# Attention and a squared-ReLU MLP in one kernel: v read as fp32 by SyncE's queue and cast on GpSimd, weight sums on GpSimd, batch 2's x turned by DMA

## The chip, the cores and the metric

The kernel runs on one core of a Trainium2 chip. The metric is device time in microseconds for one execution; lower is better. Engines are called as in the profile: PE (TensorE, matrix products; PEld is its loading of weights), DVE (VectorE), ACT (ScalarE), POOL (GpSimd), SP (SyncE, which here only issues DMAs).

## The reference, cut to what matters

```python
B, H, S, D = 8, 8, 576, 64
scores = q @ k.T / sqrt(D) + bias[bucket(|i - j|)]       # per batch and head, 576 x 576
attn   = exp(scores) / sum(exp(scores))
x      = (attn @ v)            -> 4608 tokens x 512
h      = maximum(x @ w_in, 0)                             # 512 -> 2048
out    = (h * h) @ w_out                                  # 2048 -> 512, fp32
```

All inputs and the output are fp32 in memory; the kernel computes in fp16 with fp32 accumulation.

## The kernel before, in words

**Attention.** Work goes by *pairs*: pair p = 4·b + hp is two heads of batch b, 32 pairs in all. `pair` does one. q and k of both heads are turned so that the head's 64 values lie on partitions (for batches 0 to 2 by PE, L608, with a copy out of PSUM, L570 on ACT or L572 on DVE; from batch 3 on by DMA transposes of SP's queue, L591). Scores come from L653 (four key tiles, 512 queries), L677 (last 64 queries) and L702 (last 64 keys); the last two need `qz`, small zero-padded copies made on POOL or DVE (L635). ACT takes the exponentials (L664, L687, L712). The bias enters as a factor: DVE multiplies the exponentials near the diagonal by a table of exp(bias) (`tb_sb`, `tm_sb`; L745, called the bands). PE then multiplies by v (L781, L788, into the one PSUM bank `pv`), in two halves of three and two query tiles; v carries a column of constants so that the row sums come along. DVE takes a reciprocal (L805) and scales (L810) into `x`. x is turned into `xt` for the next layer: for batches 0 to 2 by PE, four tiles into a bank (`x_turn`, L848) and a copy; from batch 3 on by DMA.

**MLP.** Tokens go in nine groups g of 512 (`layers`). Layer 1 is 16 *atoms* of four 128x512 products (L1044, called f1 here), each with a ReLU (L1065 on ACT, L1067 on DVE) and a square (L1075, DVE). Layer 2 of a group (`second`, L962) is a 2x2 block product done with seven products in place of eight, 14 atoms of eight 128x256 products. It needs sums of the activations' blocks (L921, DVE) and sums of w_out's blocks, made once (`sums_of_weights`, L901, eight DVE instructions of 128x1024, the results in `wt_sb` and in place in `w_out_sb`). Results leave through `y` and SP's queue (L1015).

**Loads.** q, k, v and the weights come through POOL's DMA queue, which casts fp32 to fp16 on the way (L271). v of batch 0 comes by heads (`load_v_head`), of the others by token tiles (`load_v`), always as fp16 straight into `va` (tokens 0 to 511) and `vm` (the last 64). Only pair 0's q and k come as fp32 over SP's and ACT's queues into the room of a later buffer, `first_f`, and are cast by ACT and DVE.

**Order.** Everything is recorded in a planner (`Plan`). Each operation has a time it is estimated to take, a due time, buffers (`Ring`, with so many slots) and earlier operations it depends on. The planner fixes the order of each engine's queue before the kernel runs: of what could start earliest it takes what is due first. `nominal(p)` is a pair's due time, `G0` and `GP` give the groups' due times, `AHEAD` says how early a pair may begin. On the chip each engine runs its list in order and waits on semaphores, so the planner's times matter only through the order that they make. Operations put down as `DMA` are transfers that the planner expects, not instructions.

Of the kernel before, what the change touches and what calls it, by code (L numbers as in the profile page):

```python
# [30 lines left out]
PERIOD, LEAD, FAST, FASTN = 9600.0, 1600.0, 3000, 7  # L31
AHEAD, G0, GP = 20600.0, 54700.0, 35900.0
DT_X = 3
RELU_DVE = 2
NSTG, NQK, NPT, NV, NX, NGB, NRT, NY = 5, 4, 3, 3, 6, 2, 4, 4
QUIET, LATER = 5200.0, 8500.0
TAB, EV = 6400.0, 1
P_ORDER = "1 6 2 5 7 3 4"
P_LAST = "1 6 2 5 7 3 4"
SIX = 3  # L40
ORDER = "k0 i0 q0 q1 v i1 i2 o0 k1 o1 i3 o2 o3"
# [149 lines left out]
def kernel(  # L191
# [38 lines left out]
    one_sb = sb("one_sb", [1, 128], FP32)  # L230
    ex_sb = sb("ex_sb", [128, 8])
    eb_sb = sb("eb_sb", [128, 4, 8])
    oh_sb = sb("oh_sb", [128, 512])
# [14 lines left out]
    gs = [sb(f"g{i}", [128, 16, GT]) for i in range(NGB)]  # L248
    rts = [sb(f"rt{i}", [128, GT]) for i in range(NRT)]
# [16 lines left out]
    def loader(eng_name, eng, out_, in_, packets, deps=(), bufs=(), due=0.0):  # L266

        lane = [Buf(r_lane)] if eng_name == "POOL" else []
        issue = P.add(
            {eng_name: 720.0 if eng_name == "POOL" else 600.0},  # L270
            lambda: io(eng.dma_start(out=out_(), in_=in_())),  # L271
            deps,
            list(bufs) + lane,
            due,
        )
        return P.add({"DMA": packets / 16}, None, [issue], list(bufs) + lane, due if lane else -1e9), issue
# [9 lines left out]
    def load(eng_name, eng, out_, in_, packets, deps=(), bufs=(), due=0.0):  # L286
        return loader(eng_name, eng, out_, in_, packets, deps, bufs, due)[0]
# [15 lines left out]
        128 * 27, due=0,  # L303
# [21 lines left out]
        {"PE": 250.0},  # L325
# [21 lines left out]
    for c in range(6):  # L347
        t_b = Buf(r_g)

        def t_mm(c=c, t_b=t_b):  # L350
            for j in range(16 * c, 16 * c + 16):
                io(
                    nc.tensor.matmul(  # L353
                        g_ps[t_b.slot][:, ts(j - 16 * c, 32)], oh_sb[:, 380 - 4 * j : 508 - 4 * j],
                        eb_sb.rearrange("p i h -> p (i h)"), start=True, stop=True,
                    )
                )

        o = P.add({"PE": 16 * 55.0}, t_mm, [o_eb, l_oh], [t_b], LEAD + TAB, 0.0, "f")

        def t_ev(o, c=c, t_b=t_b):
            src = g_ps[t_b.slot].rearrange("p (w h) -> p h w", h=H)
            dst = tb_sb[:, :, ts(c, 64)]
            if o.eng == "ACT":
                io(nc.scalar.activation(out=dst, in_=src, func=COPYF))
            else:
                io(nc.vector.tensor_copy(out=dst, in_=src))

        tabs_done.append(one_of({"DVE": dve(512), "ACT": act(512)}, t_ev, [o], [t_b], 1.0))
# [17 lines left out]
    def fill(ap, value, ns, due, after, deps=()):  # L387
# [3 lines left out]
    z_fix = [[fill(zz[:, 0], 0.0, 150.0, 10, QUIET)], [fill(zz[:, 1:], 0.0, 300.0, 11, LATER)]]  # L391
    first = [
        fill(pt_sb[:, :, PW:], 1.0, 150.0, 20, LATER),
        fill(pm_sb[:, :, S:], 1.0, 150.0, 20, LATER),
# [11 lines left out]
        fill(stg[i][w][96:128, 512:640].bitcast(FP32), 0.0, 90.0, 40 + i, 25000.0)  # L406
# [4 lines left out]


# [50 lines left out]
    def cast_first(w):  # L463

        def cast(o):
            src, dst = first_f[0:96, ts(w, 768)], stg[b_stg[0].slot][w][0:96, :]
            if o.eng == "ACT":
                io(nc.scalar.activation(out=dst, in_=src, func=COPYF))
            else:
                io(nc.vector.tensor_copy(out=dst, in_=src))  # L470

        l_qk[0, w] = [one_of({"ACT": act(768), "DVE": dve(768, 2.0)}, cast, [l_first[w]], [b_stg[0]], -3.0)]

    def load_v_head(b, h):
        l = load(
            "POOL", nc.gpsimd,
            lambda: vas[b_v[b].slot][:, :, h, 0:64],
            const(v[b, h, 0:512, :].rearrange("(t p) d -> p t d", p=128)),
            512 * 34.5, v_fix[min(b, 1)], [b_v[b]], pdue(),
        )  # L480
        l_v.setdefault((b, h // 2), []).append(l)
# [12 lines left out]
    def load_v(b):  # L494
        for tt in range(4):
            l = load(
                "POOL", nc.gpsimd,
                lambda tt=tt: vas[b_v[b].slot][:, tt, :, 0:64],
                const(v[b, :, ts(tt, 128), :].transpose([1, 0, 2])),
                1024 * 34.5, v_fix[min(b, 1)], [b_v[b]], pdue(),  # L500
            )
            for hp in range(4):
                l_v.setdefault((b, hp), []).append(l)
        load_v_tail(b)

# [22 lines left out]
    for hp in range(4):  # L528
        for w in range(2):
            if hp:  # L530
                load_six(hp, w)
            else:
                cast_first(w)
        if hp == 2:
            load_v_tail(0)
        if hp >= 1:
            for h in range(2 * hp - 2, 2 * hp):
                load_v_head(0, h)
    for h in range(6, 8):
        load_v_head(0, h)  # L540
    for step in ORDER.split():
        if step[0] == "i":
            load_w_in(int(step[1]))
        elif step[0] == "o":
            load_w_out(int(step[1]))
        elif step[0] in "qk":
            for p in range(4 + 2 * int(step[1]), 6 + 2 * int(step[1])):
                load_six(p, "qk".index(step[0]))
        else:
            load_v(1)  # L550
    for b in range(2, B):
# [3 lines left out]
        load_v(b)  # L555
# [3 lines left out]
    def nominal(p):  # L559
        return LEAD + FAST * min(p, FASTN) + PERIOD * max(p - FASTN, 0)  # L560

    xt_ready, x_last = {}, {}
# [17 lines left out]
    def pair(p):  # L580
# [5 lines left out]
        for w, dst in ((0, qts), (1, kts)):  # L586
# [14 lines left out]
            def tr(w=w, bank=bank):  # L601
                ps = g_ps[bank.slot].bitcast(FP16)
                t = stg[b_stg[p].slot][w]
                if b < SIX:
# [12 lines left out]
            o = P.add({"PE": 12 * 36.0 if b < SIX else 5 * mm(128)}, tr, l_qk[p, w] + [l_id], [bank, b_stg[p]], T - 3000, after, "c" if b < SIX else "f")  # L617
# [153 lines left out]
        for part, qt0, nq in ((0, 0, 3), (1, 3, 2)):  # L771
            bank = Buf(r_pv)

            def pv(qt0=qt0, nq=nq, bank=bank):
                ps = pv_ps[bank.slot][:, 0 : nq * 130].rearrange("p (t e d) -> p t e d", t=nq, e=2)
# [27 lines left out]
            def recip(nq=nq, bank=bank, rb=rb):  # L803
                ps = pv_ps[bank.slot][:, 0 : nq * 130].rearrange("p (t e d) -> p t e d", t=nq, e=2)
                io(nc.vector.reciprocal(out=rs[rb.slot][:, 0:nq], in_=ps[:, :, :, 64:65]))  # L805

            def norm(nq=nq, bank=bank, rb=rb, qt0=qt0):
                ps = pv_ps[bank.slot][:, 0 : nq * 130].rearrange("p (t e d) -> p t e d", t=nq, e=2)
# [29 lines left out]
    def x_turn(b, norms):  # L838
        xb = [x_bufs[4 * b + hp] for hp in range(4)]
        T = nominal(4 * b + 3)  # L840
        for qt in range(5):
            n = 128 if qt < 4 else 64
            bank = Buf(r_g)

            def tr(qt=qt, bank=bank):
                ps = g_ps[bank.slot].bitcast(FP16)
                for kk in range(4):
                    io(nc.tensor.transpose(ps[:, ts(kk, 128)], xs[xb[kk].slot][:, qt, :], id_sb))  # L848

            deps = [n_[0 if qt < 3 else 1] for n_ in norms]  # L850
            o = P.add({"PE": 4 * mm(128)}, tr, deps, [bank] + xb, T, 0.0, "f")
            t0 = (b % XB) * S + qt * 128
            for a, z in [(0, n)]:
                c = t0 + a
                e = copy_to(
                    4 * (z - a),
                    lambda a=a, z=z, c=c: xt_sb[:, :, c : c + z - a],
                    lambda a=a, z=z, bank=bank: g_ps[bank.slot].bitcast(FP16)[:, 0:512].rearrange(
                        "p (k t) -> p k t", k=4
                    )[:, :, a:z],  # L860
                    [o] + xt_free(b * S + qt * 128 + n), [bank], T,
                )
                for g_ in range((b * S + qt * 128) // GT, (b * S + qt * 128 + n - 1) // GT + 1):
                    xt_ready.setdefault(g_, []).append(e)
# [19 lines left out]
    def sums_of_weights():  # L884

        done = []
        for c0 in (0, 4):
            cs = ds(c0, 4)
            l = [l_wout[c0 // 2], l_wout[c0 // 2 + 1]]
# [3 lines left out]
            for out_, a, b_, op in (  # L893
# [6 lines left out]
                    {"DVE": dve(1024, 2.0)},  # L900
                    lambda out_=out_, a=a, b_=b_, op=op: io(nc.vector.tensor_tensor(out=out_, in0=a, in1=b_, op=op)),  # L901
                    l + [o], (), 1e5,
# [123 lines left out]
    def layers(g):  # L1026
# [4 lines left out]
        if g < NG:  # L1031
# [3 lines left out]
            for nt in range(16):  # L1035
                bank = Buf(r_g)

                def f1(nt=nt, bank=bank):
                    c = (g * GT) % XR
                    n = min(GT, XR - c)  # L1040
                    for a, z, c in ((0, n, c), (n, GT, 0)):
                        for kk in range(4 if z > a else 0):
# [11 lines left out]
        for i in range(16):  # L1054
            if i < len(atoms1):
                nt, f1, bank = atoms1[i]
                o = P.add(
                    {"PE": 4 * mm(512)}, f1, xt_ready[g] + [l_win[nt // 4]], [bank, gb1], due + i * 2000, 0.0, "f"
# [38 lines left out]
    for b in range(B):  # L1097
        norms = [pair(4 * b + hp) for hp in range(4)]
        if b < DT_X:
            x_turn(b, norms)  # L1100
# [38 lines left out]
```

The softmax here doesn't subtract the row's maximum and nothing guards it: scores larger than these inputs give would overflow.

## Time and profile before

| | |
|---|---|
| time, median of 3 runs | 377.3 us (377.29 to 378.32) |
| the profiled execution | 378.11 us |
| its span, first to last instruction | 376.3 us |
| PE busy in the span | 362.4 us |
| DVE, ACT, POOL busy | 269.0, 255.5, 178.3 us |
| first f1 product starts | 41.24 us |
| DMA packets of POOL's queue (q0) | 94496, 60.9% of 16 engines' span |
| DMA packets of SP's and ACT's queues (q1) | 51280, 27.3% |

The span is that of the instructions; the time of the execution is 1.8 us longer. [...] A window row gives, for a stretch of the span, each engine's busy time and number of instructions, the clock granted to PE, the share of DMA time and the rate. POOL's DMA rows are the issue of a transfer; the transfer itself lands some us later.

### The profile page before, as it was taken

What the parts mean: (1) busy time and instruction counts of PE and PEld (TensorE: products, weight loads), DVE (VectorE), ACT (ScalarE), POOL (GpSimd) and SP (SyncE); (2) the same over time, 40 slices, a digit from 0 to 9 for tenths busy, and PEclk for the clock granted to TensorE, in tenths of its full rate; (3) what the DMA queues carried; (4) which work ended last, traced back from release to release, by engine and by line L of the source; (5) the groups of instructions that cost most, each with busy time, mean ns of one, the idle gap of its engine ahead of it and who ended that gap; (6) DMA issues with size and microseconds to landing.
All of it is one profiled execution on the core that took longest, in us unless ns stands there. A gap on an engine that the chain in (4) does not pass through costs nothing.

```text
span 376.3 us, 10050 instructions
## 1 busy us (share of the span) xinstructions
PE 362.4 (96%) x4046; PEld 247.6 (66%) x4046; DVE 269.0 (71%) x612; ACT 255.5 (68%) x361; POOL 178.3 (47%) x318
## 2 busy tenths in 40 slices
PE   3988999999999999999999999999999999999996
PEld 2656555745778666687766765677577878556775
DVE  3987689998788677767685777757776683583653
ACT  4888979988557887866787778747885541564330
POOL 7876453889368583933758446583550000000000
PEclk9989999999999999999999999999999999999999
DMA  9999999699999999949999799999990222200103
GB/s 171 145 119 159 200 170 88 44 95 84 83 159 129 111 118 145 108 47 119 142 135 67 109 121 149 79 110 105 162 116 30 77 58 68 70 2 28 57 28 111
DMA packets 146163, 38.74 MB, mean 103 GB/s; under 512 B 128070, under 2 KB 146118, under 8 KB 146118
## 3 DMA queue, kind: packets, MB, share of 16 engines
q0 software_dynamic: 94496, 18.07, 60.9%
q1 hardware_dynamic: 51280, 19.75, 27.3%
q8 instruction: 31, 0.51, 0.6%
q10 hardware_dynamic: 342, 0.30, 0.3%
q14 instruction: 14, 0.11, 0.1%
HBM read 36.88 MB, written 9.44 MB: 123 GB/s over the span
## 4 chain that ended last, share of the span: by engine, by line
PE 90%; ACT 4%; DVE 3%; issue 1%; DMA 1%; ACTq 0%
PE f L1044 34%; PE f L962 29%; PE pv L788 10%; PE st L653 9%; PE pv L781 3%; PE st L702 2%; PE st L677 2%; ACT pt L664 1%; PE f L608 1%; DMA g<-in_k_dram 1%; ACT pt L687 1%; PE f L848 1%; DVE x L810 0%; ACT kt L570 0%; PE f L353 0%
## 5 line engine op out<-in xcount | busy, mean ns | idle before, releaser
L664 ACT ACTIVATE pt<-st 128x1024 f16<-128x1024 f32 x128 | 126.8, 1024 | 22.6 <-PE st L653 22.5
L1044 PE MATMUL f<-xt,w_in_sb 128*128 128x512 f16 (+4 forms) x704 | 142.1, 341 | 0.0
L1065 ACT ACTIVATE rt<-f 128x512 f16<-128x512 f32 x134 | 80.0, 598 | 62.0 <-PE f L1044 60.5
L1044 PEld LDWEIGHTS <-w_in_sb 128*128 128x128 f16 x704 | 62.6, 98 | 53.0 <-issue 10.8
L1075 DVE TENSOR_TENSOR g<-rt 128x512 f16<-128x512 f16 x144 | 60.7, 423 | 41.3 <-ACT rt L1065 40.2
L745 DVE TENSOR_TENSOR pt<-pt,tb_sb 128x1536 f16<-128x1536 f16 (+2 forms) x96 | 58.2, 621 | 10.6 <-ACT pt L664 10.2
L962 PEld LDWEIGHTS <-g 128*128 128x128 f16 x576 | 54.9, 98 | 15.4 <-issue 4.7
L788 PE MATMUL pv<-va,pt 128*128 128x65 f16 x1280 | 55.3, 194 | 0.0
L788 PEld LDWEIGHTS <-pt 128*128 128x128 f16 x1280 | 50.9, 98 | 2.9 <-issue 0.7
L271 POOL DMA_DIRECT2D qs<-in_q_dram x71 | 50.0, 725 | 2.4 <-DMA ks<-in_k_dram 1.1
L271 POOL DMA_DIRECT2D ks<-in_k_dram x71 | 50.0, 715 | 1.4 <-issue 1.4
L962 PEld LDWEIGHTS <-s 128*128 128x128 f16 x432 | 40.6, 98 | 10.6 <-issue 3.4
L635 POOL COPY qz<-qt 64x64 f16<-64x64 f16 x53 | 15.5, 293 | 64.2 <-DMA qt<-qs 35.5
L989 DVE SCALAR_TENSOR_TENSOR y<-f,y 128x512 f32<-128x512 f32 (+1 forms) x47 | 31.4, 667 | 16.1 <-PE f L962 15.1
L653 PE MATMUL st<-qt,kt 64*128 64x512 f16 x256 | 41.6, 396 | 1.1 <-ACT pt L664 0.5
L962 PE MATMUL f<-wt,g 128*128 128x256 f16 x288 | 36.6, 273 | 0.0
L962 PE MATMUL f<-w_out_sb,s 128*128 128x256 f16 x288 | 36.6, 273 | 0.0
L962 PE MATMUL f<-w_out_sb,g 128*128 128x256 f16 x288 | 36.2, 273 | 0.1
L781 PE MATMUL pv<-vm,pm 128*128 128x130 f16 x160 | 35.5, 222 | 0.5 <-DVE x L810 0.4
L635 POOL COPY qz<-kt 64x64 f16<-64x64 f16 x59 | 20.2, 342 | 33.3 <-DMA kt<-ks 17.4
L810 DVE TENSOR_TENSOR x<-pv,r 128x384 f16<-128x384 f32 x64 | 31.4, 490 | 1.9
L271 POOL DMA_DIRECT2D va<-in_v_dram x36 | 30.8, 860 | 1.5 <-DMA qs<-in_q_dram 0.8
(62 smaller groups left out, 308.0 us busy)
## 6 DMA issues: line engine op xcount, KB each, us to landing
out_dram<-y SPq DMA_DIRECT2D x34, 256.0 KB, 2.4
va<-in_v_dram POOLq DMA_DIRECT2D x28, 128.0 KB, 4.7
qs<-in_q_dram POOLq DMA_DIRECT2D x40, 64.0 KB, 3.2
ks<-in_k_dram POOLq DMA_DIRECT2D x40, 64.0 KB, 3.0
w_in_sb<-in_moe_w_in_dram POOLq DMA_DIRECT2D x4, 512.0 KB, 7.6
w_out_sb<-in_moe_w_out_dram POOLq DMA_DIRECT2D x4, 512.0 KB, 9.9
qs<-in_q_dram POOLq DMA_DIRECT2D x11, 144.0 KB, 5.0
ks<-in_k_dram POOLq DMA_DIRECT2D x11, 144.0 KB, 6.2
```

The source lines that it names most:

```text
L271: lambda: io(eng.dma_start(out=out_(), in_=in_())),
L635: io(eng.tensor_copy(out=dst[qb.slot][rw, rw], in_=src[qb.slot][rw, 512:576]))
L653: nc.tensor.matmul(sets_ps[st.slot][:, e, :], kt[rw, ts(jt, 128)], qt[rw, 0:512], start=True, stop=True,)
L664: nc.scalar.activation(out=p5(pts[pb.slot])[:, jt, :, 0:512], in_=sets_ps[st.slot], func=EXPF, scale=SCALE)
L745: io(nc.vector.tensor_tensor(out=a, in0=a, in1=t, op=MULT))
L781: nc.tensor.matmul(ps[:, i, :, :], pm[:, c : c + 128], vm[:, hp, :, 0:65], start=True, stop=False)
L788: nc.tensor.matmul(ps[:, i, e, :], pt[:, (2 * jt + e) * S + c : (2 * jt + e) * S + c + 128], va[:, jt, 2 * hp + e, 0:65], start=False, sto ...
L810: nc.vector.tensor_tensor(out=xs[xb.slot][:, qt0 : qt0 + nq, :].rearrange("p t (e d) -> p t e d", e=2), in0=ps[:, :, :, 0:64], in1=rs[rb.s ...
L962: nc.tensor.matmul(g_ps[bf.slot][:, ts(s_, HALF)], left(c, s_), right(c), start=(c == 0 and (s_ == 0 or apart) and i not in before), stop= ...
L1044: nc.tensor.matmul(g_ps[bank.slot][:, a:z], w_in_sb[:, kk, ts(nt, 128)], xt_sb[:, kk, c : c + z - a], start=(kk == 0), stop=(kk == 3),)
L1065: io(nc.scalar.activation(out=rts[rb.slot], in_=g_ps[bank.slot], func=RELUF))
L1075: nc.vector.tensor_tensor(out=gs[gb1.slot][:, nt, :], in0=rts[rb.slot], in1=rts[rb.slot], op=MULT)
```

## The change

- **v.** All batches' v is read as fp32 by SP's queue and cast by a POOL `tensor_copy` into `va` and `vm`. Batches 0 and 1 (`fetch_v`) go through the free room behind `first_f`, batches 2 to 7 (`load_v_fp32`) through two small buffers `fs`. Other POOL loads wait for the first two casts (`GATE`).
- **Weight sums.** `sums_of_weights` becomes 16 POOL instructions of 128x512 in place of eight DVE instructions of 128x1024.
- **x.** Batches 0 and 1 are turned by PE pair by pair (three and two tiles); batch 2 is turned by DMA like the later ones (`DT_X` 3 to 2). The first three f1 atoms of group 0 are split: three of their four products need only pairs 0 to 2 (`PRE`).
- **Start.** Pair 0 is cast into another order and turned with six transposes of 96x128 in place of twelve of 96x64 for each of q and k; the constants' memsets are allowed at once (`QUIET`, `LATER`, `FILL`); the copies of the turned q and k of pairs 1 to 4 are for DVE alone (`EV`); the bias' one-hot table lies in a buffer that is free then.
- **Planner.** Due times and estimates change, the loads of the weights are ordered anew (`ORDER`), layer 2's products run as 1 2 6 5 7 3 4 in all groups but the last.

```diff
-PERIOD, LEAD, FAST, FASTN = 9600.0, 1600.0, 3000, 7
-AHEAD, G0, GP = 20600.0, 54700.0, 35900.0
-DT_X = 3
-RELU_DVE = 2
-NSTG, NQK, NPT, NV, NX, NGB, NRT, NY = 5, 4, 3, 3, 6, 2, 4, 4
-QUIET, LATER = 5200.0, 8500.0
-TAB, EV = 6400.0, 1
-P_ORDER = "1 6 2 5 7 3 4"
+PERIOD, LEAD, FAST, FASTN = 9500.0, 2400.0, 3000, 8
+AHEAD, G0, GP = 25000, 60000, 46000
+DT_X = 2
+RELU_DVE = 3
+NSTG, NQK, NPT, NV, NX, NGB, NRT, NY, NF = 5, 4, 3, 3, 6, 2, 4, 4, 2
+QUIET, LATER = 1100.0, 800
+TAB, EV = 6700.0, 5
+P_ORDER = "1 2 6 5 7 3 4"
...
-ORDER = "k0 i0 q0 q1 v i1 i2 o0 k1 o1 i3 o2 o3"
+PV_G, PRE, FILL = 0, 3, 1100.0
+V0_AT, V1_AT, V1_LAT, GATE = 3000.0, 12400.0, 12000.0, 2
+T_DUE = 0
+V_EARLY, V_SW = 21800.0, 8
+ORDER = "i0 k0 q0 k1 q1 i1 o0 i2 i3 o1 o2 o3"
...
+        if eng_name == "POOL" and due > 6.0:
+            deps = list(deps) + v_cast[0:GATE]
...
+    def fetch_v(b):
+        rb = Buf(r_room)
+        for tt in range(4):
+            l = load(
+                "SP", nc.sync,
+                const(room_f[:, ts(tt, 512)].rearrange("p (h d) -> p h d", h=H)),
+                const(v[b, :, ts(tt, 128), :].transpose([1, 0, 2])),
+                1024 * 19, (), [rb], -0.5 + b, after=(V0_AT, V1_AT)[b], turn=6.5 + 3 * b,
+            )
+            o = P.add(
+                {"POOL": 780.0},
+                lambda tt=tt: io(
+                    nc.gpsimd.tensor_copy(
+                        out=vas[b_v[b].slot][:, tt, :, 0:64],
+                        in_=room_f[:, ts(tt, 512)].rearrange("p (h d) -> p h d", h=H),
...
+    def load_v_fp32(b):
+
+        due, at = pdue(), max(0.0, nominal(4 * b) - V_EARLY)
+        for tt in range(5):
+            fb = Buf(r_f)
...
+            for room, src, dst, packets, ns in parts:
+                l = load("SP", nc.sync, room, const(src), packets, (), [fb], due, after=at, turn=due)
+                o = P.add(
+                    {"POOL": ns},
+                    lambda room=room, dst=dst: io(nc.gpsimd.tensor_copy(out=dst(), in_=room())),
+                    [l] + v_fix[1], [fb, b_v[b]], due,
+                )
...
-    def x_turn(b, norms):
...
-            def tr(qt=qt, bank=bank):
-                ps = g_ps[bank.slot].bitcast(FP16)
-                for kk in range(4):
-                    io(nc.tensor.transpose(ps[:, ts(kk, 128)], xs[xb[kk].slot][:, qt, :], id_sb))
+    def x_turn(p, norms):
...
+            def tr(qt0=qt0, nq=nq, bank=bank):
+                ps = g_ps[bank.slot].bitcast(FP16)
+                for i in range(nq):
+                    io(nc.tensor.transpose(ps[:, ts(i, 128)], xs[xb.slot][:, qt0 + i, :], id_sb))
...
-        for c0 in (0, 4):
-            cs = ds(c0, 4)
-            l = [l_wout[c0 // 2], l_wout[c0 // 2 + 1]]
+        for c0 in range(0, 8, 2):
+            cs = ds(c0, 2)
+            l = [l_wout[c0 // 2]]
...
-                    {"DVE": dve(1024, 2.0)},
-                    lambda out_=out_, a=a, b_=b_, op=op: io(nc.vector.tensor_tensor(out=out_, in0=a, in1=b_, op=op)),
-                    l + [o], (), 1e5,
+                    {"POOL": 1150.0},
+                    lambda out_=out_, a=a, b_=b_, op=op: io(nc.gpsimd.tensor_tensor(out=out_, in0=a, in1=b_, op=op)),
+                    l + [o], (), T_DUE,
...
+                ahead = 3 if g == 0 and i < PRE else 0
+                o = None
+                if ahead:
+                    o = P.add(
+                        {"PE": ahead * mm(512)}, lambda f1=f1: f1(k1=3),
+                        [x for kk in range(ahead) for x in xt_pair[g, kk]] + [l_win[nt // 4]], [bank, gb1],
+                        due + i * 2000, 0.0, "f",
+                    )
```

## The prediction

> **What bounds the kernel now.** I read the page's busy shares and slices first, then windows cut at the first f1 product and at the last layer-2 stretch, then the timeline at the cuts.
>
> ```profile
> PE 362.4 (96%) x4046; PEld 247.6 (66%) x4046; DVE 269.0 (71%) x612; ACT 255.5 (68%) x361; POOL 178.3 (47%) x318
> ...
> PE   3988999999999999999999999999999999999996
> ```
>
> ```profile
> 0.00:41.20 41.20, 31.44 (x542) 21.64 (x542) 29.44 (x89) 32.11 (x44) 32.34 (x61) 0.96 1.22 153
> 41.20:362.00 320.80, 320.36 (x3413) 216.92 (x3412) 233.83 (x513) 222.21 (x317) 145.92 (x257) 1.00 0.88 98
> 362.00:376.30 14.30, 10.57 (x96) 8.99 (x93) 5.76 (x10) 1.15 (x2) 0.00 (x0) 0.98 0.22 73
> ...
> 5.00:20.00 15.00, 13.37 (x222) 8.91 (x222) 12.90 (x39) 12.07 (x17) 12.81 (x24) 1.00 1.43 161
> 20.00:41.00 21.00, 17.87 (x324) 12.73 (x321) 16.27 (x50) 18.47 (x26) 15.63 (x29) 0.92 1.21 146
> 41.00:66.00 25.00, 24.98 (x293) 13.21 (x290) 21.60 (x47) 21.94 (x33) 9.11 (x15) 1.00 1.09 146
> ```
>
> After the window come its length and the busy time of PE, PEld, DVE, ACT, POOL. From 41.2 to 362 us PE is idle for 0.44 of 320.8 us: that stretch is a sum of PE instructions, and no faster load or helper engine shortens it. Before 41.2 us PE has 542 of its 4046 products in 31 busy us, slowly fed, while DVE (12.90 of 15) and ACT (18.47 of 21) are near full. The last 14.3 us are one group's layer 2 and its stores. So the time is 41.2 + 320.8 + 14.3, and the change can act on the first term, or put waits into the second.
>
> ```profile
> 20.62 2.15 DVE L745 TENSOR_TENSOR pt<-pt,tb_sb 128x1536 f16<-128x1536 f16 x3
> 21.75 0.29 PE L781 MATMUL pv<-vm,pm 128*128 128x130 f16 x1
> 40.32 0.45 PE L848 MATMUL f<-id_sb,x 128*128 128x128 f16 x5 [0.57 <-DVE x L810]
> 41.24 0.39 PE L1044 MATMUL f<-xt,w_in_sb 128*128 128x512 f16 x1
> ```
>
> Start, duration, instruction, in brackets the idle time and its end. The first product with v stands at 21.75 us, right behind DVE's bands; the first f1 at 41.24 us, behind x of pair 3 and its turning, with PE idle for 0.57 us ahead of the last five transposes.
>
> [...]on POOL's small copies:
>
> ```profile
> L635 POOL COPY qz<-kt x59: 229/235/1030, 8.3 to 281.2; 64x64 f16<-64x64 f16 x59
> ...
> 51.31 1.39 DVE L745 TENSOR_TENSOR pt<-pt,tb_sb 128x1536 f16<-128x1536 f16 x2
> 51.43 1.37 POOL L635 COPY qz<-kt 64x64 f16<-64x64 f16 x2 [8.24 <-ACT kt L570]
> ```
>
> Least, median and most are 229, 235 and 1030 ns; two copies that start beside a band take 1.37 us. [...] Before, POOL has only copies of 64 elements[...].
>
> **The change, part by part.**
>
> *First product with v.* Of what DVE does between 5.3 and 21.6 us, memsets are 2.41 us (ten groups in the timeline); they move into the first 5 us, where DVE is idle but for 0.17 us. Ten `qz` copies (2.12 us) become four (0.92). Two more copies of turned q or k out of PSUM stand ahead of it in the new order, 2 x 0.75 us. One small band (0.25) falls behind. Sum: -2.41 - 1.20 + 1.50 - 0.25 = -2.4 us, so 19.4 us, as DVE was nearly never idle there. v must be ready by then: in POOL's new order the casts of batch 0 stand behind the `qz` copy of pair 3, whose q DVE delivers by about 12.9 us (6.6 us of its work from 5.3, and the 1.0 us it idled before). From there POOL has two `qz` copies (0.5), [...]one w_in issue (0.76) and one k issue (0.72)[...]. The six v loads are issued by SP from 2.1 us on at 0.42 us each (row of `oh_sb`), idle time of SP.
>
> *From there to f1.* ACT sheds five evacuations of 0.65 us (3.3 us) up to pair 3, so it doesn't bind instead. x is turned pair by pair, and nine f1 products (9 x 0.216 = 1.9 us) need no pair 3; they fill the wait of 0.57 us and the turning behind it. I take 1.4 us for this; 0 to 1.9. Against it: loads of pairs 4 to 7 now stand behind the casts. Pair 5's k is issued at some 19.5 us and lands 5.0 to 6.2 us later (the page's rows of issues of 144 KB), 24.5 to 25.7; PE reaches its turning near 23.6 us by the new order. A wait there of 1 to 2 us is partly beside DVE's chain; I take 0.6. Start: 2.4 + 1.4 - 0.6 = 3.2 us gained, between 0.5 (all eaten by loads) and 6 (ACT's 3.3 also comes through).
>
> *Turning batch 2 by DMA.* PE loses 20 transposes:
>
> ```profile
> L848 PE MATMUL f<-id_sb,x x60: 216/219/230, 38.1 to 120.7; 128*128 128x128 f16 x60
> ```
>
> [...]in the timeline they follow each other at 55 ns (five in 0.45 us). 20 x 0.055 and five starts are 1.2 us off the packed stretch: all gained. SP gets eight transposes of 1.2 us; they land in 3.4 us, and their f1 come many us later. DVE and ACT lose five copies of some 0.5 us, which gain nothing there.
>
> *v.* POOL drops 52 issues (va 30.8 us, vm 10.0 us busy)[...]. The DMA engines move 256-byte rows without a cast. SP gets 48 issues of 0.42 us. Neither POOL (47%) nor the DMAs release PE in the packed stretch, so this is worth nothing by itself. What it adds: q, k issues and `qz` copies queue on POOL behind casts that wait for a landing; behind the `qz` copies are the scores of L677 and L702. Pairs may begin about 2.5 planned pairs ahead, which hides a few us.
>
> *Weight sums.* DVE drops eight of 0.69 us (5.5 us, off the path). POOL gets 16[...]. They stand behind the `qz` copy of pair 7, whose k ACT delivers near 38 us[...]. PE's new order needs them at layer 2's product 6 of group 0, at PE work that the old kernel reached at 70 us, so at 66.4 us now. [...]each may wait for a DVE band or sum. I take 0.8 us for waits[...] in all; 0 to 8. A gain below 0 is excluded, since PE had nothing to gain there.
>
> *Planner and product order.* The seven products are the same; changes of kind on PE are 115 after the first f1 (before: 117). Attention ends earlier in the order, f1 and layer 2 fill the rest. Nothing; -1 to +1 us. The tail is untouched.
>
> Sum: -3.2 - 1.2 + 0.8 = -3.6 us on the profiled execution of 378.11 us, which gives 374.5. That one lay 0.8 us above the median of 377.3, so **373.7 us**. A measurement of this kernel can tell about 0.3%, 1.1 us, from no change.
>
> **Rivals.**
>
> 1. *The sums come late and PE waits (slower).* For it: POOL runs in order, sat idle for 16 us between 41 and 66 us before, and its copies took up to 1.03 us against 0.235[...].[...] If each of 16 sums waits for half a band (0.45 us), that is 7.2 us[...]. It decides once the sums end after 72 us (66.4 + 4.4 + 1.1). Chance 0.14.
> 2. *The start doesn't move.* Pair 5's load or v's casts replace DVE as what ends last[...]. Only the 1.2 us of transposes remain: 376.1 us. For it: DMA share is 1.43 in 5 to 20 us. Chance 0.12.
> 3. *DVE becomes the bound.* [...]between 41 and 66 us it was busy for 21.6 of 25, so 3.4 us are free[...]. Against it: its list is otherwise shorter. Chance 0.08.
>
> **How the numbers follow.** The forecast has 0.66: its own range is 370 to 376, from the start's bounds. Rival 2 lies half beyond -0.3%. So faster 0.72, same 0.10, slower 0.18. The range 369.8 to 379.0 takes in rivals 2 and 3 and leaves the late sums and an even better start out.
>
> **What would show it.** Right: first product with v near 19.5 us, first f1 near 38 us, no L848 of batch 2, PE idle under 2 us from then to the tail[...]. Wrong: PE waits on POOL ahead of layer 2 of group 0, DVE bands or squares visibly longer than 0.95 and 0.42 us, PE waiting for q or k loads at 24 us, or a first f1 still at 41 us.

## The result, and the profile after

| | before | after |
|---|---|---|
| median of 4 runs | 377.49 us (377.29 to 378.32) | 392.76 us (388.92 to 395.98) |
| the profiled execution, its span | 378.11, 376.3 us | 393.85, 392.1 us |

The ratio is 1.0366 [1.0283, 1.045]: the change makes the kernel slower by 3.7%, and the forecast of 373.7 us, with its range of 369.8 to 379.0, missed it. One of the change's four runs (395.98 us) was a slow one and is left out of the ratio; the other three have a median of 391.7 us, from which the experiments below are counted.

PE's busy time and its slices, from the page of the kernel after:

```profile
PE 365.8 (93%) x4014; PEld 248.5 (63%) x4014; DVE 287.8 (73%) x624; ACT 250.0 (64%) x353; POOL 181.1 (46%) x319
...
PE   4989696599999799999999999999999999999996
```

A slice is 9.8 us. Before, the nines began at the fifth slice and held to the last but one. Now there are holes in slices 5, 7 and 8 and one in slice 14. The windows put a size on them (columns as in the prediction's windows: length, busy time of PE, PEld, DVE, ACT, POOL, PE's clock, DMA share, rate):

```profile
20.00:41.00 21.00, 18.99 (x352) 13.07 (x349) 19.19 (x53) 18.94 (x27) 8.41 (x14) 1.00 1.19 196
41.00:66.00 25.00, 18.46 (x127) 9.14 (x126) 18.51 (x27) 13.43 (x21) 23.87 (x33) 0.86 0.86 135
66.00:100.00 34.00, 29.45 (x422) 20.75 (x422) 32.01 (x70) 22.70 (x34) 25.13 (x36) 0.90 0.74 86
...
120.00:140.00 20.00, 17.26 (x186) 11.36 (x185) 13.04 (x28) 12.34 (x18) 12.22 (x25) 0.91 0.97 145
```

From 41 to 66 us PE is busy for 18.46 of 25 us and runs 127 products; before it was 24.98 us and 293. POOL, with 9.11 us there before, has 23.87. Two more holes follow. PE's granted clock falls to 0.86 to 0.91 in just these windows, which adds to the loss: sixteen products right behind the longest wait take 3.60 us at a granted clock of 0.50, sixteen like them six us later 1.91 at 1.00.

```profile
73.97 3.60 PE L1047 MATMUL f<-w_out_sb,g 128*128 128x256 f16 x16
...
79.73 1.91 PE L1047 MATMUL f<-w_out_sb,g 128*128 128x256 f16 x16
```

PE's waits name what ended each hole (us in total, times, longest):

```profile
PE f L692 <- DVE rt L1161: 4.2, 1, 4.2
PE st L789 <- POOL qz L722: 3.4, 1, 3.4
PE f L1129 <- DVE rt L1161: 3.2, 2, 1.7
PE f L1129 <- DMA xt<-x: 2.6, 1, 2.6
```

Before, none of these four was there. They are three different things, read below one by one.

**First hole: 44 us, POOL.** POOL's casts of batch 1's v (`va<-g`) and the scores that wait for `qz`, from the timelines of POOL and PE:

```profile
31.84 0.77 POOL L528 CAST va<-g 128x512 f16<-128x512 f32 x1 [4.34 <-DMA g<-in_v_dram]
...
38.41 0.62 POOL L528 CAST va<-g 128x512 f16<-128x512 f32 x1 [5.24 <-DMA g<-in_v_dram]
...
44.63 0.66 PE L789 MATMUL st<-qt,qz 128*128 128x288 f16 x2 [3.40 <-POOL qz L722]
```

POOL works in order. It stands idle for 4.34 and 5.24 us ahead of casts whose data have not landed, and the weights' loads, the `qz` copies and the sums queue up behind. SP's queue shows why the data are late:

```profile
2.15 11.84 SPq L281 DMA_DIRECT2D g<-in_v_dram  x6
14.04 2.32 SPq L281 DMA_DIRECT2D f<-in_v_dram  x2
16.48 18.78 SPq L281 DMA_DIRECT2D g<-in_v_dram  x6
```

The six loads of batch 0 occupy SP for 11.84 us and the six of batch 1 for 18.78, some 2 and 3 us each in the mean where the forecast had 0.42; and two 256 KB loads of batch 2 (`f`) stand between them.

**Second hole: 60 to 73 us, DVE.** DVE's timeline where PE waits, with relu (L1161), square (L1169) and sums of activations (L1006); then POOL's sums of the weights in the same time:

```profile
57.32 1.40 DVE L1169 TENSOR_TENSOR g<-rt 128x512 f16<-128x512 f16 x1
58.75 1.53 DVE L1006 TENSOR_TENSOR s<-g 128x1024 f16<-128x1024 f16 x1
60.20 1.37 DVE L1169 TENSOR_TENSOR g<-rt 128x512 f16<-128x512 f16 x1
61.49 0.68 DVE L1161 TENSOR_SCALAR rt<-f 128x512 f16<-128x512 f32 x1
...
62.23 1.89 PE L1129 MATMUL f<-xt,w_in_sb 128*128 128x512 f16 x8 [1.45 <-DVE rt L1161]
```

```profile
L986 POOL TENSOR_TENSOR wt<-w_out_sb 128x512 f16<-128x512 f16 x8 | 10.1, 1260 | 0.4
```

A square takes up to 1.4 us in place of 0.42, a sum of activations 1.5 to 1.6 in place of 0.69; a relu keeps its 0.68. One POOL sum takes 1.26 us in the mean of these eight, and DVE's operations beside it take about as long. PE needs a PSUM bank that a relu must empty first, and the relu stands behind the stretched squares and sums of activations: 1.45 and 1.72 us of waits ahead of f1, and 4.18 ahead of the turning of a later pair's k (L692).

**Third hole: 136 us, SP's queue.** An f1 product waits for a turned x:

```profile
135.79 0.54 PE L1129 MATMUL f<-xt,w_in_sb 128*128 128x512 f16 x1 [2.60 <-DMA xt<-x]
```

The turn that it waits for was issued at 130.09 us, behind two v loads of SP that occupy it for 1.15 us from 128.84 on, and behind other turns.

### The profile page after: what moved, and what is told of

It is laid out like the page before. It is cut to its first block, busy times and chain, and to the rows that moved or that the text cites. A ratio compares the mean times of both kernels' runs of the same rounds, so it can differ in the third digit from the quotient of the medians.

```text
span 392.1 us, 10088 instructions
## 1 busy us (share of the span) xinstructions
PE 365.8 (93%) x4014; PEld 248.5 (63%) x4014; DVE 287.8 (73%) x624; ACT 250.0 (64%) x353; POOL 181.1 (46%) x319
## 4 chain that ended last, share of the span: by engine, by line
PE 81%; DMA 8%; DVE 7%; POOL 2%; issue 1%; ACT 0%; POOLq 0%
PE f L1129 30%; PE f L1047 28%; PE pv L875 8%; PE st L740 7%; DMA g<-in_v_dram 4%; DVE g L1169 3%; PE pv L868 2%; PE st L789 2%; DVE s L1006 2%; PE st L764 1%; DMA xt<-x 1%; PE f L692 1%; DMA g<-in_k_dram 1%; DMA ks<-in_k_dram 1%; DVE rt L1161 1%
## 5 line engine op out<-in xcount | busy, mean ns | idle before, releaser
L1129 PE MATMUL f<-xt,w_in_sb 128*128 128x512 f16 (+4 forms) x704 | 146.6, 345 | 5.8 <-DVE rt L1161 3.2
L1159 ACT ACTIVATE rt<-f 128x512 f16<-128x512 f32 x126 | 75.1, 598 | 75.1 <-PE f L1129 71.9
L1169 DVE TENSOR_TENSOR g<-rt 128x512 f16<-128x512 f16 x144 | 69.9, 489 | 45.4 <-ACT rt L1159 44.1
L1129 PEld LDWEIGHTS <-w_in_sb 128*128 128x128 f16 x704 | 63.8, 99 | 53.9 <-issue 15.3
L832 DVE TENSOR_TENSOR pt<-pt,tb_sb 128x512 f16<-128x512 f16 (+2 forms) x96 | 59.3, 635 | 7.5 <-ACT pt L751 6.9
L1047 PEld LDWEIGHTS <-s 128*128 128x128 f16 x432 | 40.8, 98 | 10.5 <-issue 1.7
L740 PE MATMUL st<-qt,kt 64*128 64x512 f16 x256 | 41.2, 394 | 1.6 <-ACT pt L751 1.2
L1047 PE MATMUL f<-w_out_sb,g 128*128 128x256 f16 x288 | 37.3, 281 | 0.1
L722 POOL COPY qz<-qt 64x64 f16<-64x64 f16 x50 | 14.5, 290 | 38.9 <-DMA qt<-qs 26.8
L591 POOL CAST va<-f 128x512 f16<-128x512 f32 x24 | 17.0, 719 | 21.7 <-DMA f<-in_v_dram 21.4
L1006 DVE TENSOR_TENSOR s<-g,s 128x1024 f16<-128x1024 f16 x36 | 26.7, 742 | 0.4
## 6 DMA issues: line engine op xcount, KB each, us to landing
g<-in_v_dram SPq DMA_DIRECT2D x8, 256.0 KB, 10.5
```

The costliest lines, as they stand in the source:

```text
L740: nc.tensor.matmul(sets_ps[st.slot][:, e, :], kt[rw, ts(jt, 128)], qt[rw, 0:512], start=True, stop=True,)
L832: io(nc.vector.tensor_tensor(out=a, in0=a, in1=t, op=MULT))
L1006: io(nc.vector.tensor_tensor(out=out_, in0=a, in1=b_, op=mybir.AluOpType.subtract))
L1047: nc.tensor.matmul(g_ps[bf.slot][:, ts(s_, HALF)], left(c, s_), right(c), start=(c == 0 and (s_ == 0 or apart) and i not in before), stop= ...
L1129: nc.tensor.matmul(g_ps[bank.slot][:, a:z], w_in_sb[:, kk, ts(nt, 128)], xt_sb[:, kk, c : c + z - a], start=(kk == 0), stop=(kk == 3),)
L1159: io(nc.scalar.activation(out=rts[rb.slot], in_=g_ps[bank.slot], func=RELUF))
```

## The experiments

Each ratio is to runs of the kernel before on the same chip (medians 377.3 to 378.2 us). What comes back is counted from the change's 391.7 us (the expectations count from 392.8). The change's three runs lie between 388.9 and 393.9 us, so a return of less than some 3 us isn't clear by time alone. In kernels with a line more, line numbers are one or a few higher. "Lock theory" in the expectations is the author's name for a guess: that POOL's sums and DVE's operations with two SBUF inputs hold each other up, after squares of up to 1.40 us beside sums of 1.15 to 1.48 us in the change.

### Each part taken out of the changed kernel

**e1: the sums on VectorE, in the same places.**

```diff
-io(nc.gpsimd.tensor_tensor(out=out_, in0=a, in1=b_, op=op))
+io(nc.vector.tensor_tensor(out=out_, in0=a, in1=b_, op=op))
```

> The changed kernel with the 16 sums of w_out's blocks issued on DVE at the same place of the recorded order; all else as it was. Lock theory: [...]without them the squares go back from up to 1.4 us to 0.42 us, the idle times of PE ahead of ReLUs on DVE (1.45, 1.72 and 4.18 us between 62 and 74 us) vanish, and the kernel gains 6 to 8 us: 385 to 387 us. Theory that v of batch 1 lands late and that this alone costs the time: the stall at 41 to 45 us stays and under 2 us are gained. Theory that the planner's new order is at fault: within 2 us of 392.

385.88 us, 1.0194 [1.0156, 1.0232]: 5.8 us come back. The squares have a mean of 448 ns again and the waits for relu go. The 3.4 us for `qz` and 2.8 us for a turned x stay, so these two holes have another cause.

**e2: v of batch 1 by POOL's queue, cast on the way, as before.**

```diff
-    fetch_v(1)
+        else:            # step "v" of ORDER, after q1
+            load_v(1)
```

> The changed kernel with v of batch 1 loaded through POOL's casting queue again (six loads after the loads q1). Late-v theory: SP's loads of batch 1 are issued from 16.5 to 35.3 us and POOL's casts wait 4.3, 5.2 and 1.0 us for them, with qz copies behind; PE's wait of 3.4 us at 44.6 us and the slow stretch from 40 to 50 us go, 4 to 6 us gained, and the sums start some 8 us earlier: 386 to 389 us. Lock theory alone: the stall of 60 to 75 us only moves earlier, under 2 us gained.

387.13 us, 1.0245 [1.0208, 1.0282]: 4.5 us. The wait for `qz` is gone, and so is the one for the turned x at 120 to 140 us. A wait for relu (3.1 us) stays, with 4.2 us for x from DVE.

**e3: v of batches 2 to 7 by POOL's queue.**

```diff
-V_EARLY, V_SW = 21800.0, 8
+V_EARLY, V_SW = 21800.0, 2
```

> The changed kernel with v of batches 2 to 7 loaded through POOL's casting queue again; batches 0 and 1 still by SP. If SP's queue with v of later batches costs time in the steady stretch: the loss of 4 us between 120 and 140 us goes, 3 to 5 us gained, 388 to 390 us. If v of later batches is hidden: within 1.5 us of 392.8.

389.59 us, 1.0297 [1.025, 1.0344]: 2.1 us, within the spread. The wait for `qz` shrinks to 1.3 us and the one for the turned x to 0.4.

**e4: x of batch 2 turned by PE again.**

```diff
-DT_X = 2
+DT_X = 3
```

> The changed kernel with x of batch 2 turned by PE again, pair by pair. If batch 2's DMA transposes come late to the third group's f1 (2.6 us of wait for xt at 135.8 us): the loss between 120 and 140 us goes, some 3 us gained less 1.2 us for the transposes, 390 to 391 us. If turning by DMA is the gain that was forecast: 1 to 1.5 us slower, 394 us.

391.67 us, 1.0361 [1.0335, 1.0387]: no return. That wait for x goes here too, so three different parts can each remove it.

**e8: all weight loads but the first held back until v of batch 1 is cast.**

```diff
-                512 * 102, (), (), pdue(),
+                512 * 102, v_cast[0:11] if after_v1 else (), (), pdue(),
```

> The changed kernel with all weight loads but the first moved behind v of batch 1: its casts are no longer in competition with 2 of 8 weight loads (2 MB read). If the DMA engines are full from 5 to 40 us and that is why v of batch 1 lands at 38 to 40 us: its last cast comes 3 to 5 us earlier, PE's wait for qz at 44.6 us shrinks, but f1 of the fifth and later atoms waits for w_in; in sum within 3 us of 392.8. If SP's own order (two loads of batch 2 ahead of batch 1) or the freeing of the room is what delays it: the casts stay where they were.

388.64 us, 1.0288 [1.0243, 1.0333]: 3.0 us. v's last cast ends at 37.1 us in place of 41.9, and no product waits for `qz`. But a hole closed early opens a later one: PE's longest waits after the start are now

```profile
PE pv L877 <- DVE pt L834: 4.9, 1, 4.9
PE f L694 <- DVE rt L1163: 3.6, 1, 3.6
PE f L1131 <- DMA xt<-x: 3.2, 1, 3.2
```

since the sums start at 45.8 us and meet the bands too. The weights' traffic was part of what delayed v.

### Why do the sums on GpSimd cost so much?

**e6: the kernel before, with only its sums moved to POOL (16 of 512 elements, due at once).**

```diff
-                    {"DVE": dve(1024, 2.0)},
-                    ... io(nc.vector.tensor_tensor(out=out_, in0=a, in1=b_, op=op)),
-                    l + [o], (), 1e5,
+                    {"POOL": 1150.0},
+                    ... io(nc.gpsimd.tensor_tensor(out=out_, in0=a, in1=b_, op=op)),
+                    l + [o], (), 0,
```

> The kernel before with one part of the change alone: the sums of w_out's blocks as 16 POOL instructions of 128x512, due at once. Lock theory: DVE's squares and sums of activations are stretched while POOL sums (some 45 to 66 us), and the kernel is 4 to 7 us slower, 382 to 385 us. Late-v theory[...]: within 1.5 us of 377.8.

388.63 us, 1.0291 [1.0251, 1.0331]: +10.5 us, more than the 4 to 7 that the lock theory had. No fp32 v is in it, so the sums alone make the kernel slower. They end at 63.4 us, ahead of the 66.4 us at which the forecast needs them, and no product waits for one. Bands of 512 to 1536 elements have a mean of 1267 ns from 40 to 75 us, squares 690.

**e7: e1, and in place of each sum four memsets of an unused tile on POOL.**

```diff
+    idle_sb = sb("idle", [128, 352])
-io(nc.vector.tensor_tensor(...))
+(io(nc.vector.tensor_tensor(...)), [io(nc.gpsimd.memset(idle_sb, 0.0)) for _ in range(4)])
```

> The changed kernel with the sums issued on DVE, and in each one's place on POOL four memsets of an unused 128x352 tile, which read nothing. It keeps POOL occupied without reading SBUF. Lock theory: as with the sums on DVE alone, 384 to 387 us, squares at 0.42 us. If it is POOL's occupation that delays what is queued behind the sums (q and k loads, casts): as slow as the changed kernel, 390 to 394 us, by as much as the memsets take of the sums' 20 us.

392.31 us, 1.0373 [1.0312, 1.0434]. By its time alone this run would say that POOL's occupation is all. The trace says otherwise. DVE's squares between 49 and 75 us, first of the change, then of e7:

```profile
L1169 DVE TENSOR_TENSOR g<-rt 128x512 f16<-128x512 f16 x13 | 13.0, 1010 | 0.2
```

```profile
L1170 DVE TENSOR_TENSOR g<-rt 128x512 f16<-128x512 f16 x13 | 5.5, 421 | 0.2
```

The 64 memsets (391 ns each, 25.0 us) leave the squares at 421 ns in the mean. They hold POOL's list until 80.4 us, 8 us longer than the sums did, and so a load of k is late:

```profile
83.58 0.69 PE L693 MATMUL f<-id_sb,ks 96*64 96x96 f16 x12 [4.84 <-DMA ks<-in_k_dram]
```

That wait is absent in the change. So a busy POOL can cost by what queues behind it, as in e7, or by what it does to DVE beside it. The second is what the change shows. What holds the two engines up, no run shows; the traces show which operations it meets. Beside the sums the change's squares took up to 1.40 us (before: 0.42) and its sums of activations 1.53 to 1.64 (0.69), and e6's bands had a mean of 1.27 us, where the longest before took 0.96: all have two SBUF inputs. Five relus (PSUM in) beside the change's sums took 0.68 to 0.69 us, as elsewhere, and squares beside the memsets 0.42.

### Do the parts add up? Each part alone on a clean kernel

**e5: the changed start and v of batch 0 as changed; sums on VectorE, v of all other batches by POOL's queue.**

```diff
-PV_G, PRE, FILL = 0, 3, 1100.0
+PV_G, PRE, FILL = 0, 2, 1100.0
-V_EARLY, V_SW = 21800.0, 8
+V_EARLY, V_SW = 21800.0, 2
-    fetch_v(1)                           # and load_v(1) after q1
-io(nc.gpsimd.tensor_tensor(...))
+io(nc.vector.tensor_tensor(...))
```

> The changed kernel with three parts undone at once: sums of w_out on DVE, v of batch 1 and of batches 2 to 7 through POOL's casting queue; two f1 atoms split in place of three, as the planner finds no order else. What stays of the change: v of batch 0 by SP, the start, x of batch 2 by DMA, the planner's due times. Apart, the three parts gained 6.9, 5.6 and 3.2 us; if these are three separate stalls, they add up, 377 us; if stalls share their place (both v parts lost the stretch 120 to 140 us), 379 to 381 us. If the start and the 20 transposes bring what was forecast (4.4 us), below 375 us.

379.74 us, 1.0051 [1.0036, 1.0066]. (Six f1 products go ahead here, nine in the change.) 12.0 us come back, about what the three parts gave one by one (5.8, 4.5 and 2.1); the forecast's gain of 4.4 us for start and transposes isn't there. The next four are e5 with one part put back (or one more taken out).

**e9: e5 with `DT_X = 3`.** 

> The variant with v of batch 0 alone as fp32 (379.7 us), and x of batch 2 turned by TensorE again. What then differs from the kernel before is the start alone (constants, v of batch 0, the order around it). If the 20 transposes are worth what the forecast gave them (1.2 us), this one takes about 381. If the turn by DMA costs, through its place in SyncE's queue, as the 1.1 us between the changed kernel and its own variant with the turn on TensorE suggests, it takes 378.6. If the start has its forecast 3.2 us and something in the DMA turn eats them, it takes 374 to 375.

381.52 us, 1.0112 [1.0086, 1.0138]. Turning x of batch 2 by DMA is worth 1.8 us here (0.6% by the ratios, with some 0.3% of uncertainty), not a loss. What is left, the new start with v of batch 0, the planner's new order and the sums early on DVE, is 4 us slower than before.

**e10: e5 with `V_SW = 8`.** 

> The same variant with v of batches 2 to 7 as fp32 through SyncE's queue, cast by GpSimd: this part alone added to 379.7 us. If the parts add up, it costs the 3.2 us that taking it out of the changed kernel gave back: 383, with TensorE waiting for a turned x near 120 to 140 us. If the forecast's zero holds without the congestion of the other parts: 379 to 380.5.

378.98 us, 1.0044 [1.0027, 1.006]. v of batches 2 to 7 costs nothing here: the forecast's zero.

**e11: e5 with `fetch_v(1)` again and no step "v".** 

> The same variant with v of batch 1 as fp32 ahead of the weights: this part alone added to 379.7 us. If the parts add up, it costs the 5.6 us that taking it out of the changed kernel gave back: 385, with GpSimd's casts held until near 40 us, the scores of a pair waiting over 3 us for qz behind them, and 4 us lost between 40 and 50 us. If the late casts only hurt in the company of the sums on GpSimd: 380 to 382.

380.41 us, 1.0085 [1.0064, 1.0106]: 0.7 us, not 5.6.

**e12: e5 with the sums on POOL.** 

> The same variant with the 16 sums of layer 2's weights on GpSimd: this part alone added to 379.7 us. If the parts add up: 6.9 us (as taken out of the changed kernel) to 10.5 us (as added to the kernel before), 386.5 to 390, with VectorE's squares beside them at 1.0 us and more in place of 0.42. If the sums cost mainly because the late v of batch 1 pushed them onto the first squares: 380 to 383, since here they can begin at 53 us at the latest and the weights that they read land by then.

388.47 us, 1.0287 [1.0266, 1.0308]: 8.7 us, though the order of the lists is that of e5 and only the issuing engine differs. PE's longest waits between 36 and 82 us are for DVE, where e5 has none for a relu and 0.7 us for a band:

```profile
PE f L1130 <- DVE rt L1162: 4.6, 1, 4.6
PE pv L876 <- DVE pt L833: 4.1, 1, 4.1
```

The sums are dear in any company; the two parts of v are dear only together: alone +0.7 and -0.8 us, together 6.1 (e1 less e5). With the sums on POOL it is the same: 388.5 us with neither part (e12), 389.6 with batch 1 alone (e3), 387.1 with the later batches alone (e2), 391.7 with both (the change). That e1 puts nine f1 products ahead and e5 six isn't the reason, as e2 and e3 put nine ahead too and stay near e12.

### What makes the two parts of v dear together?

**e13: the change, with v of batch 2 behind v of batch 1 in SP's queue.**

```diff
-        due, at = pdue(), max(0.0, nominal(4 * b) - V_EARLY)
+        due, at = pdue(), max(40000.0, nominal(4 * b) - V_EARLY)
```

> The changed kernel, with v of batch 2 issued behind v of batch 1 in SyncE's queue (in the changed kernel two of its 256 KB loads go ahead, at 14.04 and 14.69 us); all else as changed. If these two loads are why v of batch 1 is late: GpSimd's casts end near 36 us in place of 41, the wait of 3.4 us for qz goes, and 3.2 to 5.6 us come back (387 to 389.5; these are what taking v of batches 2 to 7, or of batch 1, off this queue gave). If the weights' and q's loads on the other queue are what delays v of batch 1: no change, 391 to 394.

389.57 us, 1.0321 [1.0299, 1.0343]: 2.1 us come back, within the spread. SP's queue in the new order, and the fourth cast of batch 1:

```profile
2.15 23.84 SPq L282 DMA_DIRECT2D g<-in_v_dram  x12
26.04 7.70 SPq L282 DMA_DIRECT2D f<-in_v_dram  x2
```

```profile
34.18 0.68 POOL L529 CAST va<-g 128x512 f16<-128x512 f32 x1 [4.02 <-DMA g<-in_v_dram]
```

The last cast ends at 38.1 us in place of 41.9, and the wait for `qz` is 0.7 us. It still waits for its data, so the order was a part, not the whole.

**e14: e13 with the sums on VectorE.** 

> The same order of SyncE's queue, and the sums on VectorE in the places that they have on GpSimd. The order theory: v of batch 1 and of the later batches then cost together what they cost alone (0.7 and -0.7 us on 379.7), 379.5 to 381.5. The rival, that fp32 traffic of all batches costs by its amount: 384 to 386, as with the sums alone moved (385.9).

382.2 us, 1.0139 [1.011, 1.0169]: 3.7 us below e1 (2.1 by the ratios, give or take 1.8), 2.5 above e5. Of the 6.1 us that both parts of v cost together, some 2 to 4 are the order of SP's queue. The rest is in neither theory's numbers; waits of 2.7 us for a band and 1.6 us for k are in the trace, but no run isolates them.

### Where do the earlier start's 2 us go?

**e15: e10 with the sums due late on VectorE, as before.**

```diff
-T_DUE = 0
+T_DUE = 1e5
-                    {"POOL": 1150.0},
+                    {"DVE": dve(512, 2.0)},
```

> v of batch 1 by GpSimd's queue and of batches 2 to 7 as fp32 (379.0 us), with the sums of the weights on VectorE and due late, as in the kernel before, in place of due at once. The theory: the earlier start's 2 us are lost because VectorE, at 4.9 us of each 5 between 55 and 75 us, holds the products, and 16 sums of 0.42 us stand there (before they ran at 74 to 95 us); so 2 to 3 us come back, 376 to 377. The rival: the loss between 55 and 75 us comes from the order of the heads' small products and stays: 378.5 to 379.5.

376.51 us, 0.9975 [0.9965, 0.9986]: 2.5 us below e10, and 0.9 us faster than the kernel before, the best version of the study. Windows of the kernel before, of e10 and of e15:

```profile
55.00:75.00 20.00, 19.89 (x306) 13.16 (x305) 19.02 (x48) 18.54 (x29) 11.90 (x25) 1.00 0.83 69
```

```profile
55.00:75.00 20.00, 15.44 (x255) 11.39 (x254) 19.56 (x50) 14.04 (x21) 4.71 (x7) 1.00 0.41 43
```

```profile
55.00:75.00 20.00, 18.11 (x310) 12.71 (x310) 19.21 (x43) 15.92 (x24) 11.68 (x21) 1.00 0.72 86
```

DVE is nearly full in all three, with 19.02, 19.56 and 19.21 of 20 us; before, PE lost only 0.1 us beside it. In e10 PE idles for 4.6 us, 4.3 of them ahead of x from DVE: in this stretch DVE is the bound. With the 16 sums of 0.44 us spread from 46 to 103 us, PE gets 2.7 us back.

**e16: e14 with the sums due late on VectorE.** 

> The whole change but for the sums, which are on VectorE and due late, with v of batch 2 behind v of batch 1 in SyncE's queue. If order and the sums' place are all that was wrong with the change: 376.5 to 379. If fp32 v costs by its traffic: over 382.

380.58 us, 1.0103 [1.0081, 1.0126], 1.6 us below e14 and between its two theories. A wait of 1.7 us for a turned x in SP's queue is back.

**e17: e15 with the sums on POOL, also due late.**

```diff
-io(nc.vector.tensor_tensor(...))
+io(nc.gpsimd.tensor_tensor(...))
```

> The variant of 376.5 us (sums on VectorE, due late) with the sums on GpSimd, also due late, spread between its other work. If the place was wrong (in a row ahead of the first squares, at 49 to 72 us) and not the engine: 374.5 to 377, since VectorE loses 6.7 us of work while it is the bound. If the engine is wrong, because each sum stretches VectorE's two-input operations beside it (0.42 to 1.0 or 1.4 us, at 1.2 to 1.5 us of sum each): some 16 x 0.6 = 10 us more of VectorE's time, partly on the path: 379 to 385.

386.12 us, 1.0219 [1.0196, 1.0243]: +9.6 us on e15, a little more than the range expected of a wrong engine, although only ten of the 16 sums run before 62 us. It is the engine, not the place. The squares from 40 to 100 us:

```profile
L1170 DVE TENSOR_TENSOR g<-rt 128x512 f16<-128x512 f16 x25 | 17.3, 705 | 0.2
```

## Why the prediction was wrong

One path of runs adds the parts one after the other, each number a difference of medians:

| step | kernels | us |
|---|---|---|
| new start, v of batch 0, its order, sums early on DVE | before to e9 | 377.5 to 381.5: +4.0 |
| x of batch 2 by DMA | e9 to e5 | 379.7: -1.8 |
| v of batches 1 to 7 by SP, cast on POOL | e5 to e1 | 385.9: +6.1 |
| sums on POOL | e1 to after | 391.7: +5.8 |

By each kernel's ratio to the kernel before on its own chip the four steps are +4.2, -2.3, +5.4 and +6.5 us.

*First product with v at 19.4 us: wrong.* It came at 21.50 (before: 21.75). The step that failed is that DVE "was nearly never idle there" and so set it. The memsets did move (DVE is busy 3.07 us in the first 5 us, and 11.36 of the next 15, before 12.90), but the time that they freed there stayed idle. Both kernels put 32 score products ahead of the first with v, and the last of them wait for exponentials on ACT, which runs without a gap from 16.2 us (before: from 15.7). The forecast took the DVE band that ends beside this product for what releases it; PE's row just ahead of it, in the kernel before and then after, names ACT, and PE has no idle time between the two:

```profile
20.71 1.10 PE L653 MATMUL st<-qt,kt 64*128 64x512 f16 x4 [0.53 <-ACT pt L664]
```

```profile
20.69 0.88 PE L740 MATMUL st<-qt,kt 64*128 64x512 f16 x4 [0.53 <-ACT pt L751]
21.50 0.23 PE L868 MATMUL pv<-vm,pm 128*128 128x130 f16 x1
...
38.35 0.82 PE L1129 MATMUL f<-xt,w_in_sb 128*128 128x512 f16 x3
```

*First f1 near 38 us: right* (38.35), by another way than the sum said, and partly by luck. This f1 doesn't wait for pair 3 any more, whose last turning starts at 39.00 us (before: 40.32). And just behind the first product with v PE ran faster: eight products took 0.41 us, before 0.65, but in e15 0.64 again, so this isn't the change's doing. *v of batch 0 ready in time: right*, its last cast ended at 18.9 us, with 0.61 us a cast of 512 elements here and 0.72 later; no trace of before had shown what such a cast takes. *The start worth 3.2 us: wrong.* A first f1 some 3 us earlier moved PE's work forward into a stretch where DVE is full (55 to 75 us). The stretch after 41.2 us was read as a sum of PE instructions, but DVE had been busy for 21.6 of 25 us there, 3.4 us short of full. The sums, put early, used that up (2.5 us, e15). The rest of the start's gain is lost too: in e15, with DVE at 19.21 of 20 us, PE still idles for 1.9 us between 55 and 75 us, before 0.1. How much of that is the planner's new order, which the forecast put at nothing, no run isolates.

*Twenty transposes, 1.2 us: right* on the clean kernel (1.8), with nothing to see in the change's company (e4).

*v at nothing: wrong in its company.* Alone each part is nearly free (+0.7, -0.8). The failed step is "48 issues of 0.42 us". The price came from a row of one small load. With three loads of 1024 pieces of 256 bytes not yet landed (batch 1's first four took 10.1 to 19.5 us from issue to landing), an issue kept SP for 6.64 us, the longest of all, so the loads behind it were issued late (what holds such an issue, no run isolates), and two loads of batch 2 ahead of batch 1's are 2 to 4 us. The forecast did say that `qz` and loads queue behind casts that wait, and that this hides "a few us"; it had no time of landing for it.

*Sums at 0.8 us: wrong by 5 to 10 us, the largest term.* Its pieces were measured. The start: 49.02 us, not just after 38, behind the late casts (40.1 in e12, where batch 1 has none). The length: 1.29 us in the mean of all sixteen, and they ended at 72.4 us; no trace of before had shown what a sum on POOL takes. There is no gap ahead of them: the last `qz` copy ends at 48.94 us, two MODIFY_POOL_CONFIG records follow, and the first sum starts at 49.02. And the stall, the step that failed: the forecast let the sums wait for DVE, with half a band each. It was DVE that waited for the sums: 13 squares took 13.0 us in place of 5.5, the sums of activations twice their time, so DVE lost over 10 us where it had 3.4 to spare.

*The rivals.* The loss has the sign of rival 1 (sums end after 72 us) but not its mechanism: no product waits for a sum, and e6 and e12, whose sums end at 63.4 us, lose 10.5 and 8.7 us. The mechanism is that of rival 3 (DVE becomes the bound). Rival 3 had the right place, DVE's 3.4 free us between 41 and 66 us; it was given 0.08 because DVE's list "is otherwise shorter". Rivals 1 and 3 had to be taken as one case, with all the sums (20.6 us as measured) beside DVE's fullest stretch, and then with more weight than all others.

## What to carry to other kernels

Before moving two-input work to GpSimd, find VectorE's fullest stretch and charge VectorE up to the whole length of each moved operation there. Here VectorE lost some 11 us beside 20.6 us of moved sums, which would have taken it 6.7 us itself; the loss lay in its operations with two SBUF inputs (eleven squares beside a sum: 1.37 us in the median, in place of 0.42). Price an in-order queue of loads by the data ahead in it, not only by the issue (two loads of batch 2 ahead of batch 1's: 2 to 4 us here); two harmless parts that share such a queue must be costed together. When the start of a kernel moves, look at the engine that is nearly full just behind it.

## What the runs showed of the hardware

- Beside POOL's sums (1.15 to 1.48 us each) DVE operations with two SBUF inputs take longer: the eleven squares of the change that overlap one have a median of 1.37 us, 0.41 the least and 1.40 the most, where squares of the kernel before have a mean of 0.42. Beside memsets on POOL (0.39 us each) squares keep 0.42 us in the mean. So do squares beside issues of DMAs on POOL: 46 of the kernel before that had only such issues beside them have a median of 0.42 us. Casts on POOL, which read SBUF, lie between: 18 squares of the change overlap one and take 0.41 to 0.88 us.
- SP's issue of a load with 256-byte pieces had no single price here. The twelve `g` loads of the change, least, median, most in ns:

```profile
L281 SPq DMA_DIRECT2D g<-in_v_dram x12: 437/1724/6642, 2.2 to 34.7; - x12
```
